# A linear attention followed by a mixture of adapters: one hand-written order of work replaced by another

## The chip, the core and the metric

The kernel runs on one core of a Trainium2 chip. A core has a matrix engine (PE, TensorE), a vector engine (DVE), an engine for functions (ACT, ScalarE), a general engine (POOL, GpSimd) and a queue engine (SP, SyncE). Each takes its own instructions strictly in order, and they meet through semaphores. Sixteen DMA engines carry data between device memory and SBUF; TensorE writes its results to PSUM, which DVE and ACT read. The metric is the device time of one execution in microseconds (us).

## What is computed

Eight batches of eight heads, 576 positions, 64 features. Queries and keys go through relu and are weighted by the cosine and the sine of their position; each head sums `kv = k_p^T v` and `z = sum k_p`, and each query row divides its numerator by its denominator. The 4608 rows of 512 then go through eight small adapters, of which the two with the highest logits count for each row.

```python
q_p, k_p = phi(q, cos_w, sin_w), phi(k, cos_w, sin_w)   # [r*c, r*s], r = max(x, 0)
kv  = einsum('bhsf,bhsd->bhfd', k_p, v)
den = einsum('bhsf,bhf->bhs', q_p, k_p.sum(2)) + 1e-6
x   = (einsum('bhsf,bhfd->bhsd', q_p, kv) / den[..., None]).transpose(0, 2, 1, 3).reshape(4608, 512)
logits = x @ w_gate                    # the top two of 8, softmax over the two: w
out = x + sum_k w[k] * (x @ A[e_k]) @ B[e_k]
```

## The kernel before

The 4608 rows are cut into 36 tiles of 128 rows, numbered n = 0 to 35; nine tiles cover two batches, and the tile in the middle of each nine (n = 4, 13, 22, 31) takes half its rows from each of the two. Batch 0 is done ahead of the order below. All else is issued one step at a time from the string `ORDER` (line 31 on): a letter names the step, numbers say which tile, batch or group, and a letter at the end (`a`, `d`, `p`) puts it on ACT, DVE or POOL. A step's instructions go to the ends of their engines' queues, so the string fixes the order on every engine at once.

For each batch b there are load steps `Dk.b`, `Dv.b`, `Dq.b` (line 131 and 140; DMAs issued by POOL, which cast f32 to bf16; a k or v comes in two parts, one of 320 KB and one of 256 KB, a q in one of 576 KB). `K b.s.i` (lines 266, 268) weights one fifth of the keys by cosine (i = 0) or sine (i = 1) on ACT or DVE. `U` (line 281) is a relu of keys on DVE for later `G b.s`, which weights on POOL with two instructions (line 271). `M b.s` (line 306) are the eight products of a fifth of a batch into `kv`, and `W b` (line 314) copies the finished `kv` out on ACT.

For each tile n: `Q` transposes the queries and weights them by cosine and sine with products against diagonal matrices (line 339, 16 products; for tiles in the list `QUAD`, line 327, 32 products of 64 by 64 that lie side by side in the quadrants of the array). `E n.gp` evacuates them with a relu on ACT (line 355) or DVE (line 357). `N` makes numerators and denominators (line 383). `R` normalises on DVE: the reciprocal (line 398) and the product (line 405). The small epsilon comes in by a product on PE, or, for tiles in `EPS_DVE`, by an addition on DVE (line 394), or, for tiles in `EPS_ACT`, by step `F` on ACT (line 366). `X` transposes the tile (line 413), `C` copies it out of PSUM on ACT or DVE (line 420), `L` multiplies it by gate and adapters (line 440). Three tiles share a gate: `A` finds the two highest logits (DVE, lines 449 to 473), `S` makes the weights (ACT), `B` applies them (DVE, line 503), `Z` transposes (line 515), and the result comes out with a `C` or with `Y` (line 520). `O` multiplies by the second adapter matrix (line 546); x itself is added by a product with the identity (line 545), or, for tiles in `ADDS`, on POOL (`P`, line 553), or, for `ADDS_DVE`, on DVE as the output is copied out. `V` copies the output out on ACT (line 564) or DVE (line 567). `T` stores it (line 577, issued by SP). `H` is a product that computes nothing used, `J` lays the adapter matrices.

Three things hold the order together across engines. The result of `N` has one PSUM place, so the next `N` waits for `R`. Buffers of keys, values and queries are used again by later batches (batch 5 takes those of batch 0 or 1, and so on), so a load waits for the last reader of the older batch. And SP, whose queue holds the stores alone, begins with one small DMA (line 625) that waits until all loads but the last `HOLD` = 2 are there; all stores stand behind it. Finished outputs wait in 24 buffers.

Of the kernel before, what the change touches and what calls it, by code (L numbers as in the profile page):

```python
# [25 lines left out]
ORDER = """
R0 H Q1.0 Q1.1 E1.0.a H X0 K1.0.1.d E1.1.a K1.1.0.d Q2.0 K1.4.0.d C0.a N1 K1.0.0.d E2.0.a
K1.2.0.d Q2.1 R1 E2.1.a H Q3.0 K1.3.0.a K1.3.1.d H N2 E3.0.d X1 K1.2.1.a Q3.1 R2 E3.1.a H H M1.3
K1.4.1.a C1.d M1.0 M1.2 K1.1.1.a N3 M1.4 R3 X2 M1.1 C2.a Q4.0 Q4.1 E4.0.a E4.1.d W1 H H H Q5.0
Q5.1 E5.0.d N4 E5.1.a X3 R4 Q6.0 Q6.1 E6.0.a C3.d H H N5 E6.1.a J Q7.0 K2.4.0.a R5 Q7.1 X4
E7.0.a L0 U2.0.2 C4.a N6 K2.3.1.d L1 G2.0 E7.1.a R6 L2 X5 K2.4.1.a Q8.0 Q8.1 A0 C5.a N7 G2.1
E8.0.a M2.4 R7 S0 M2.0 E8.1.a X6 Dq.3 K2.2.0.a M2.1 B0 N8 Dk.4 K2.3.0.a L3 R8 L4 L5 K2.2.1.a Z0
M2.3 C6.a.0 A1 Q9.0 Q9.1 M2.2 E9.0.d Dv.4 S1 E9.1.a X7 B1 Q10.0 W2 Q10.1 C7.d E10.0.a N9 X8 O0
F9 E10.1.a U3.0.2 Z1 L6 R9 O1 C8.a.1 G3.0 Q11 V0.d V1.a L7 N10 E11.0.a U3.2.3 G3.1 X9 R10 O2
E11.1.a O3 C9.a Q12.0 Q12.1 V2.d Dq.4 V3.a X10 N11 E12.0.a K3.3.1.d M3.0 G3.2 R11 K3.3.0.a M3.1  # L40
L8 E12.1.a M3.3 K3.4.0.d Dk.5 K3.4.1.a A2 M3.2 N12 M3.4 C10.d S2 F12 Q13.0 W3 B2 Q13.1 Dv.5 X11
R12 E13.0.a Z2 O4 E13.1.a O5 C11.d.2 Q14.0 V5.a N13 V4.d E14.0.a Q14.1 L9 Dq.5 K4.4.0.d F13
E14.1.a O6 R13 X12 L10 K4.4.1.a Q15 U4.0.2 C12.a N14 V6.d O7 G4.1 E15.0.a X13 R14 E15.1.a L11
Q16.0 V7.a Q16.1 G4.0 A3 C13.a N15 M4.1 E16.0.a X14 R15 E16.1.a M4.4 Dk.6 Q17.0 S3 C14.a Q17.1
B3 N16 E17.0.a X15 U4.2.3 L12 E17.1.a Dq.6 R16 O8 M4.0 C15.a G4.2 L13 K4.3.1.a V8.d Z3 L14 N17
Y3.a A4 Q18.0 K4.3.0.a Q18.1 Dv.6 M4.2 E18.0.a R17 M4.3 S4 E18.1.a X16 B4 Q19.0 W4 Q19.1
K5.4.1.d C16.a N18 U5.2.3 O9 U5.0.2 O10 E19.0.a G5.2 L15 R18 L16 E19.1.a X17 Q20.0 C17.a Q20.1
K5.4.0.d G5.1 V9.d N19 E20.0.a L17 X18 E20.1.a V10.d Z4 Q21.0 F19 G5.0 C18.a.4 Q21.1 R19 M5.4
M5.1 E21.0.a A5 N20 E21.1.a Dk.7 O11 F20 M5.2 K5.3.0.d V11.a R20 X19 O12 K5.3.1.a M5.0 V12.d S5
N21 C19.a M5.3 B5 F21 Q22 W5 R21 X20 L18 E22.0.a O13 K6.4.0.d L19 E22.1.a U6.2.4 Q23.0 U6.0.2  # L50
C20.a N22 V13.d G6.1 E23.0.a Q23.1 O14 R22 L20 E23.1.a Q24.0 Q24.1 Dv.7 A6 E24.0.a X21 Z5
E24.1.a N23 C21.d.5 Q25.0 S6 F23 Q25.1 G6.2 B6 E25.0.a O15 X22 R23 E25.1.a L21 Q26.0 C22.a Q26.1
G6.0 V14.d E26.0.a N24 X23 E26.1.a R24 Z6 O16 L22 C23.a.6 Dq.7 Q27 V16.d N25 V15.a G6.3 L23 R25
X24 K6.4.1.a M6.0 M6.1 E27.0.a P15 A7 M6.2 C24.a O17 E27.1.a N26 U7.2.4 X25 V17.a R26 M6.3 G7.3
S7 C25.a M6.4 Q28.0 W6 B7 Q28.1 T0 X26 K7.4.1.d E28.0.a N27 U7.0.2 T1 O18 E28.1.a Z7 R27 G7.0
O19 L24 V18.a T2 Q29.0 C26.a.7 Q29.1 V19.d T3 N28 G7.1 O20 E29.0.a T4 L25 R28 L26 E29.1.a O21 T5
X27 V20.a Q30.0 G7.2 C27.d Q30.1 T6 V21.a A8 N29 X28 E30.0.a T7 M7.3 C28.a R29 P17 M7.1 T8
E30.1.a M7.2 S8 T9 K7.4.0.d O22 P18 N30 B8 V22.a X29 T10 M7.0 R30 C29.a P20 M7.4 T11 Q31 W7 L27
T12 L28 E31.0.a P21 L29 T13 Z8 E31.1.a A9 Q32.0 N31 Y8.a T14 P22 E32.0.a Q32.1 R31 O23 T15 O24
E32.1.a X30 T16 S9 Q33.0 V23.a C30.d N32 B9 E33.0.a T17 P23 X31 R32 Q33.1 C31.a T18 O25 L30  # L60
E33.1.a V25.d Z9 T19 X32 V24.a N33 C32.d.9 Q34.0 T20 F33 P24 Q34.1 R33 E34.0.a L31 T21 L32 O26
E34.1.a A10 T22 X33 V26.a N34 Q35 C33.a T23 R34 P26 O27 S10 E35.0.a T24 O28 E35.1.a B10 X34 T25
N35 V27.a C34.d L33 V28.a R35 Z10 L34 T26 Y10.a O29 A11 X35 T27 V29.a O30 C35.d T28 O31 S11
V30.a B11 L35 V31.a Z11 A12 O32 T29 Y11.a V32.d S12 O33 T30 B12 O34 V33.a T31 V34.d Z12 Y12.a
T32 O35 V35.d T33 T34 T35
"""


# [1 line left out]
def kernel(ctx, tc, q, k, v, w_gate, A, Bw, out):  # L70
# [317 lines left out]
    def normalise(n):  # L388
        nd = nd_t.pop(n)[:, :, 0:4 * W].rearrange("p g (j x) -> p g j x", x=W)
        rden = p_g.tile([128, H], FP32, name="rden")  # L390
        den = nd[:, :, :, D:W]
        if n in EPS_DVE:
            den1 = p_g.tile([128, 2, 4, 1], FP32, name="den1")
            nc.vector.tensor_scalar(out=den1, in0=den, scalar1=EPS, scalar2=None, op0=ALU.add)
# [277 lines left out]
```

## Time and profile before

| what | value |
|---|---|
| three timed runs | 105.49, 110.0, 110.76 us; median 110.0 |
| the profiled execution | 105.81 us, its span 103.9 us |
| granted TensorE clock, mean over the span | 0.979 |
| busy: PE, DVE, ACT, POOL | 93.8, 85.0, 85.7, 65.8 us |
| weight loads on PE | 70.7 us |
| matmul instructions | 1764 |
| DMA: loads issued by POOL | 13.84 MB |
| DMA: SP's queue (stores and k of batch 0) | 10.62 MB |

A row of a group gives line, engine, operation, tiles, count, then busy time in us and the mean of one in ns, then the idle time of the engine just before it and what ended that. A window row gives busy time and count for PE, its weight loads (PEld), DVE, ACT and POOL, then the clock, the share of the DMA engines that was busy (over 1 where packets overlap) and what they wrote in GB/s. A timeline row gives start and length.

### The profile page before, as it was taken

What the parts mean: (1) busy time and instruction counts of PE and PEld (TensorE: products, weight loads), DVE (VectorE), ACT (ScalarE), POOL (GpSimd) and SP (SyncE); (2) the same over time, 40 slices, a digit from 0 to 9 for tenths busy, and PEclk for the clock granted to TensorE, in tenths of its full rate; (3) what the DMA queues carried; (4) which work ended last, traced back from release to release, by engine and by line L of the source; (5) the groups of instructions that cost most, each with busy time, mean ns of one, the idle gap of its engine ahead of it and who ended that gap; (6) DMA issues with size and microseconds to landing.
All of it is one profiled execution on the core that took longest, in us unless ns stands there. A gap on an engine that the chain in (4) does not pass through costs nothing.

```text
span 103.9 us, 4379 instructions
## 1 busy us (share of the span) xinstructions
PE 93.8 (90%) x1764; PEld 70.7 (68%) x1764; DVE 85.0 (82%) x302; ACT 85.7 (82%) x185; POOL 65.8 (63%) x99
## 2 busy tenths in 40 slices
PE   2999989999999999999999999899999999998600
PEld 1334866777788779768897988679878888763100
DVE  5499469558989799999989899999999989979800
ACT  4359469667999998999999999799999899997600
POOL 5996342343997599649886940999779994620000
PEclk9999999999999999999999999999999999999965
DMA  2999999999999999999999999999999999999791
GB/s 31 369 235 206 201 202 200 203 195 181 203 206 198 203 206 198 199 205 206 197 203 205 197 209 199 201 197 179 176 293 389 402 396 403 386 391 365 274 375 40
DMA packets 26997, 24.74 MB, mean 238 GB/s; under 512 B 2784, under 2 KB 21856, under 8 KB 26976
## 3 DMA queue, kind: packets, MB, share of 16 engines
q0 software_dynamic: 21248, 13.84, 90.7%
q1 hardware_dynamic: 5728, 10.62, 27.4%
q8 instruction: 14, 0.23, 0.8%
q14 instruction: 7, 0.06, 0.1%
HBM read 28.85 MB, written 9.44 MB: 368 GB/s over the span
## 4 chain that ended last, share of the span: by engine, by line
PE 41%; DMA 25%; DVE 18%; POOL 5%; issue 4%; ACT 1%; DVEq 0%; POOLq 0%
DMA v<-in_v_dram 22%; PE cd L306 9%; PE qd L339 7%; PE xz L413 6%; DVE xt L405 5%; PE nd L383 5%; PE za L440 5%; PE cd L546 4%; DMA out_dram<-osb 3%; DVE osb L567 2%; DVE xT L420 2%; DVE kp L268 2%; PE cd L545 2%; PE qd L327 1%; DVE rden L398 1%
## 5 line engine op out<-in xcount | busy, mean ns | idle before, releaser
L355 ACT ACTIVATE qpT<-qd 128x512 bf16<-128x512 f32 x67 | 38.7, 621 | 2.6 <-PE qd L339 2.2
L271 POOL TENSOR_SCALAR kp<-k,tab_kv 128x512 bf16<-128x512 bf16 x38 | 25.7, 690 | 8.3 <-PE qd L339 3.7
L405 DVE TENSOR_TENSOR xt<-nd,rden 128x512 bf16<-128x512 f32 x36 | 24.9, 691 | 2.5 <-DVE rden L398 0.5
L339 PE MATMUL qd<-diag,q 128*64 128x128 bf16 x480 | 20.6, 222 | 0.1
L306 PEld LDWEIGHTS <-kp 128*128 128x128 bf16 (+1 forms) x352 | 17.3, 96 | 2.6 <-issue 0.9
L306 PE MATMUL cd<-v,kp 128*128 128x128 bf16 (+2 forms) x312 | 17.8, 214 | 0.3
L339 PEld LDWEIGHTS <-q 128*64 128x64 bf16 x480 | 14.8, 109 | 4.4 <-issue 1.7
L420 ACT COPY xT<-xz 128x512 bf16<-128x512 bf16 (+1 forms) x25 | 16.6, 665 | 1.3 <-PE xz L413 1.1
L383 PE MATMUL nd<-kvsb,qpT 128*128 128x65 bf16 (+1 forms) x320 | 15.3, 194 | 0.7 <-DVE qpT L357 0.5
L413 PE MATMUL xz<-ident,xt 128*128 128x128 bf16 x144 | 14.2, 221 | 0.5 <-DVE xt L405 0.3
L383 PEld LDWEIGHTS <-qpT 128*128 128x128 bf16 (+1 forms) x320 | 12.0, 100 | 2.3 <-DVE xt L405 0.6
L440 PE MATMUL za<-AW,xT 128*128 128x136 bf16 x140 | 12.7, 223 | 0.0
L413 PEld LDWEIGHTS <-xt 128*128 128x128 bf16 x144 | 10.1, 115 | 3.6 <-DVE xt L405 1.9
L553 POOL TENSOR_TENSOR osb<-osb,xt 128x512 f32<-128x512 f32 x9 | 10.3, 1160 | 2.6 <-ACT osb L564 2.6
L131 POOL DMA_DIRECT2D k<-in_k_dram x14 | 9.8, 701 | 2.4 <-DMA k<-in_k_dram 2.0
L266 ACT ACTIVATE kp<-k,tab_kv 128x512 bf16<-128x512 bf16 (+1 forms) x16 | 11.2, 726 | 0.1
L131 POOL DMA_DIRECT2D v<-in_v_dram x12 | 8.4, 703 | 3.6 <-DMA v<-in_v_dram 2.6
L440 PEld LDWEIGHTS <-xT 128*128 128x128 bf16 x144 | 9.5, 98 | 1.5 <-DVE xT L420 0.3
L564 ACT COPY osb<-cd 128x512 f32<-128x512 f32 x17 | 10.0, 616 | 0.5 <-PE cd L546 0.4
L586 PE MATMUL wu<-wide,ones 128*128 128x512 bf16 x24 | 7.9, 509 | 2.1 <-DVE eps_hi L195 2.1
L140 POOL DMA_DIRECT2D q<-in_q_dram x8 | 6.3, 791 | 4.0 <-DMA q<-in_q_dram 2.2
L567 DVE TENSOR_TENSOR osb<-cd,xt 128x512 f32<-128x512 f32 x13 | 8.8, 680 | 0.0
(91 smaller groups left out, 138.7 us busy)
## 6 DMA issues: line engine op xcount, KB each, us to landing
out_dram<-osb SPq DMA_DIRECT2D x36, 256.0 KB, 4.8
q<-in_q_dram POOLq DMA_DIRECT2D x8, 576.0 KB, 11.3
k<-in_k_dram POOLq DMA_DIRECT2D x7, 320.0 KB, 10.7
v<-in_v_dram POOLq DMA_DIRECT2D x6, 320.0 KB, 11.1
k<-in_k_dram POOLq DMA_DIRECT2D x7, 256.0 KB, 10.8
v<-in_v_dram POOLq DMA_DIRECT2D x6, 256.0 KB, 11.8
k0f<-in_k_dram SPq DMA_DIRECT2D x1, 1152.0 KB, 5.5
v<-in_v_dram POOLq DMA_DIRECT2D x1, 576.0 KB, 7.7
```

The lines of the kernel that those rows point to most:

```text
L131: nc.gpsimd.dma_start(out=t[pr, :, 0:n * D], in_=x)
L266: nc.scalar.activation(dst, src, AF.Relu, bias=0.0, scale=tab)
L271: nc.gpsimd.tensor_scalar(out=dst, in0=src, scalar1=tab, scalar2=1.0, op0=ALU.mult, op1=ALU.mult)
L306: nc.tensor.matmul(out=out[:, 0:W] if b and s == NJ - 1 else out, lhsT=lhsT, rhs=rhs, start=(first and g == 0), stop=(last and g == G - 1) ...
L339: nc.tensor.matmul(out=t[cols, j, 2 * gi:2 * gi + 2, :], lhsT=q_b[b][:, 2 * gp + gi, s, :], rhs=diag[:, s, i], start=(j == 0 and gi == 0), ...
L355: nc.scalar.activation(t, src, AF.Relu)
L383: nc.tensor.matmul(out=nd[pr, gg, j * W:(j + 1) * W], lhsT=qpT[:, j, pr], rhs=kv_t[b][:, h % 2, h // 2, :], start=(eps_late(n) and j == 0) ...
L405: nc.vector.tensor_tensor(out=x, in0=nd[:, :, :, 0:D], in1=rden.rearrange("p (g j) -> p g j", g=2).to_broadcast([128, 2, 4, D]), op=ALU.mult)
L413: nc.tensor.transpose(out=xz[:, c * 128:(c + 1) * 128], in_=x[:, c], identity=ident)
L420: copy(t[:, 0:c], xz[:, 0:c * 128].rearrange("p (c s) -> p c s", c=c))
L440: nc.tensor.matmul(out=za_t[g][:, i, :], lhsT=xT[:, c, :], rhs=AW[:, c, :], start=(c == 0 and i == 0), stop=(c == DCH - 1), skip_group_che ...
L567: nc.vector.tensor_tensor(out=t, in0=src, in1=xt_t.pop(n), op=ALU.add)
```

## The change

The order is replaced, and the lists that belong to it: `EPS_DVE`, `EPS_ACT`, `QUAD`, `ADDS` and `ADDS_DVE`. No function is touched. Counted over the whole string: `QUAD` goes from six tiles to four (11, 15, 22, 27, 31, 35 become 1, 30, 31, 35), `EPS_DVE` from 22 to 27, `EPS_ACT` from 8 to 3 (and `F` steps with it), tiles whose x is added without a product from 25 to 24, of which POOL adds 10 for 9. Steps on ACT and DVE: `C` from 25 and 11 to 21 and 15, `E` from 66 and 4 to 65 and 5, `K` from 16 and 16 to 17 and 15, `V` from 20 and 16 to 22 and 14. The loads come in another order; with their places among POOL's own steps:

```
before  ... Dv.5 Dq.5 G4.1 G4.0 Dk.6 Dq.6 G4.2 Dv.6 G5.2 G5.1 G5.0 Dk.7 G6.1 Dv.7 G6.2 G6.0 Dq.7 G6.3 ...
after   ... Dv.5 G4.0 G4.1 Dk.6 G4.2 Dq.5 Dk.7 Dq.6 G5.2 G5.1 G5.0 Dv.6 G6.2 G6.1 Dq.7 Dv.7 G6.0 G7.2 G6.3 ...
```

`HOLD` stays 2, so SP's small DMA now waits for the second part of v of batch 6, where it waited for the first part of k of batch 7. The diff, cut to the lists and to the stretch around the last batch:

```diff
-EPS_DVE = [2, 3, 4, 6, 8, 10, 11, 14, 15, 16, 17, 18, 22, 24, 25, 26, 27, 28, 29, 30, 31, 34]
-EPS_ACT = [9, 12, 13, 19, 20, 21, 23, 33]
-QUAD = [11, 15, 22, 27, 31, 35]
-ADDS = [15, 17, 18, 20, 21, 22, 23, 24, 26]
+EPS_DVE = [2, 4, 5, 6, 8, 10, 11, 12, 13, 14, 15, 16, 17, 18, 19, 20, 21, 22, 24, 25, 26, 27, 28, 29, 30, 31, 34]
+EPS_ACT = [9, 23, 33]
+QUAD = [1, 30, 31, 35]
+ADDS = [15, 16, 17, 18, 19, 20, 21, 23, 25, 26]
 HOLD = 2
-ADDS_DVE = [0, 2, 4, 6, 8, 9, 10, 12, 13, 14, 16, 19, 25, 32, 34, 35]
+ADDS_DVE = [0, 3, 4, 6, 8, 10, 12, 13, 14, 22, 24, 32, 34, 35]
...
-E24.1.a N23 C21.d.5 Q25.0 S6 F23 Q25.1 G6.2 B6 E25.0.a O15 X22 R23 E25.1.a L21 Q26.0 C22.a Q26.1
-G6.0 V14.d E26.0.a N24 X23 E26.1.a R24 Z6 O16 L22 C23.a.6 Dq.7 Q27 V16.d N25 V15.a G6.3 L23 R25
...
-X27 V20.a Q30.0 G7.2 C27.d Q30.1 T6 V21.a A8 N29 X28 E30.0.a T7 M7.3 C28.a R29 P17 M7.1 T8
-E30.1.a M7.2 S8 T9 K7.4.0.d O22 P18 N30 B8 V22.a X29 T10 M7.0 R30 C29.a P20 M7.4 T11 Q31 W7 L27
...
+U6.2.4 Q22.0 Q22.1 R21 G6.2 E22.0.a X20 L18 O13 E22.1.a Q23.0 C20.a U6.0.2 N22 V13.d E23.0.a
+Q23.1 G6.1 L19 R22 E23.1.a L20 Q24.0 Q24.1 Dq.7 E24.0.a A6 Z5 X21 E24.1.a N23 Dv.7 Q25.0 C21.d.5
+S6 Q25.1 F23 E25.0.a B6 O14 X22 E25.1.a R23 O15 G6.0 L21 C22.a Q26.0 Q26.1 V14.d V15.a N24 L22
...
+K6.4.1.a R25 L23 X24 M6.0 C24.a A7 O17 P15 N26 E27.1.a M6.2 R26 M6.3 S7 T0 V17.a P16 M6.4 T1
+Q28.0 B7 W6 Q28.1 K7.4.0.d T2 X25 E28.0.a U7.0.2 N27 O18 C25.d E28.1.a O19 G7.0 T3 R27 Q29.0
...
+X27 G7.1 V21.a T7 Q30 A8 C27.a N29 T8 M7.0 E30.0.a R29 P17 M7.2 S8 T9 E30.1.a X28 O22 K7.4.1.a
+M7.3 T10 B8 P18 N30 V22.d C28.a M7.1 T11 R30 L27 P19 X29 T12 Q31 C29.a M7.4 T13 E31.1.d E31.0.a
...
```

More of the change, by code (lines that the diff above doesn't have):

```diff
@@ L31 @@
 ORDER = """
[L32 to L49, printed above, removed]
@@ L50 @@
-N21 C19.a M5.3 B5 F21 Q22 W5 R21 X20 L18 E22.0.a O13 K6.4.0.d L19 E22.1.a U6.2.4 Q23.0 U6.0.2
-C20.a N22 V13.d G6.1 E23.0.a Q23.1 O14 R22 L20 E23.1.a Q24.0 Q24.1 Dv.7 A6 E24.0.a X21 Z5
-E24.1.a N23 C21.d.5 Q25.0 S6 F23 Q25.1 G6.2 B6 E25.0.a O15 X22 R23 E25.1.a L21 Q26.0 C22.a Q26.1
-G6.0 V14.d E26.0.a N24 X23 E26.1.a R24 Z6 O16 L22 C23.a.6 Dq.7 Q27 V16.d N25 V15.a G6.3 L23 R25
-X24 K6.4.1.a M6.0 M6.1 E27.0.a P15 A7 M6.2 C24.a O17 E27.1.a N26 U7.2.4 X25 V17.a R26 M6.3 G7.3
-S7 C25.a M6.4 Q28.0 W6 B7 Q28.1 T0 X26 K7.4.1.d E28.0.a N27 U7.0.2 T1 O18 E28.1.a Z7 R27 G7.0
@@ L56 @@
-O19 L24 V18.a T2 Q29.0 C26.a.7 Q29.1 V19.d T3 N28 G7.1 O20 E29.0.a T4 L25 R28 L26 E29.1.a O21 T5
-X27 V20.a Q30.0 G7.2 C27.d Q30.1 T6 V21.a A8 N29 X28 E30.0.a T7 M7.3 C28.a R29 P17 M7.1 T8
-E30.1.a M7.2 S8 T9 K7.4.0.d O22 P18 N30 B8 V22.a X29 T10 M7.0 R30 C29.a P20 M7.4 T11 Q31 W7 L27
-T12 L28 E31.0.a P21 L29 T13 Z8 E31.1.a A9 Q32.0 N31 Y8.a T14 P22 E32.0.a Q32.1 R31 O23 T15 O24
-E32.1.a X30 T16 S9 Q33.0 V23.a C30.d N32 B9 E33.0.a T17 P23 X31 R32 Q33.1 C31.a T18 O25 L30
-E33.1.a V25.d Z9 T19 X32 V24.a N33 C32.d.9 Q34.0 T20 F33 P24 Q34.1 R33 E34.0.a L31 T21 L32 O26
@@ L62 @@
[L62 to L65, printed above, removed]
+R0 H Q1 E1.0.a E1.1.d H H X0 K1.4.1.a Q2.0 K1.1.1.d N1 K1.2.0.d E2.0.a K1.3.1.d Q2.1 R1 K1.0.1.a
+Q3.0 E2.1.a K1.0.0.d C0.d H H H N2 K1.3.0.d Q3.1 R2 E3.1.a H H M1.0 K1.2.1.a E3.0.d X1 M1.3
@@ new lines @@
+K1.1.0.a K1.4.0.d M1.2 C1.d N3 X2 R3 M1.1 Q4.0 Q4.1 E4.0.a M1.4 E4.1.d W1 H Q5.0 N4 C2.a Q5.1
+E5.0.a R4 X3 E5.1.a Q6.0 C3.a H Q6.1 K2.2.0.d E6.0.a K2.4.0.d N5 X4 E6.1.a R5 Q7.0 C4.a Q7.1
+E7.0.a J H N6 U2.0.2 E7.1.a L0 R6 L1 G2.0 K2.2.1.a L2 Q8.0 Q8.1 K2.4.1.a A0 N7 G2.1 E8.0.a X5
+M2.2 R7 K2.3.1.a M2.0 S0 C5.d E8.1.a Dq.3 M2.4 B0 X6 K2.3.0.a N8 Dk.4 L3 R8 L4 L5 Z0 Q9.0 C6.a.0
+Q9.1 A1 M2.3 E9.0.a M2.1 Dv.4 E9.1.d S1 X7 W2 B1 Q10.0 Q10.1 C7.d E10.0.a N9 L6 Z1 F9 U3.0.2
+E10.1.a X8 O0 R9 G3.0 L7 C8.a.1 O1 V0.d Q11.0 V1.a Q11.1 K3.3.1.d N10 E11.0.a U3.2.3 L8 K3.4.1.d
@@ new lines @@
+O2 E11.1.a G3.2 R10 X9 V2.a O3 Q12.0 C9.a Q12.1 V3.d G3.1 N11 K3.3.0.a X10 R11 M3.2 E12.0.a M3.3
+E12.1.a Dq.4 M3.0 A2 K3.4.0.a M3.1 Dk.5 N12 C10.d S2 M3.4 B2 Q13.0 W3 Q13.1 R12 Dv.5 X11 E13.0.a
+Z2 O4 E13.1.a O5 C11.d.2 Q14.0 V5.a V4.d Q14.1 N13 E14.0.a K4.4.0.d X12 E14.1.a U4.0.2 O6 R13
+Q15.0 G4.0 C12.a Q15.1 E15.0.a L9 L10 V6.d N14 E15.1.a L11 G4.1 R14 O7 K4.4.1.a Q16.0 V7.a Q16.1
+A3 X13 E16.0.a Dk.6 N15 E16.1.a M4.4 R15 Q17.0 C13.a M4.0 S3 E17.0.a X14 U4.2.3 O8 B3 N16 C14.a
+G4.2 Q17.1 R16 K4.3.0.a L12 L13 E17.1.a X15 L14 Dq.5 V8.d M4.1 C15.a N17 K4.3.1.a A4 Dk.7 Z3
@@ new lines @@
+Q18.0 Y3.a Q18.1 R17 E18.0.a M4.2 M4.3 E18.1.a Dq.6 X16 S4 K5.4.1.d W4 Q19.0 B4 Q19.1 C16.a N18
+K5.3.0.d L15 U5.2.3 E19.0.a O9 R18 G5.2 E19.1.a X17 L16 V9.a Q20.0 C17.d Q20.1 K5.3.1.d E20.0.a
+L17 U5.0.2 O10 N19 E20.1.a G5.1 V10.d Z4 X18 K5.4.0.a Q21.0 R19 Q21.1 C18.a.4 M5.4 G5.0 M5.2 A5
+E21.0.a N20 M5.3 E21.1.a R20 O11 Dv.6 K6.4.0.a O12 M5.1 V11.a V12.d X19 S5 M5.0 C19.a B5 N21 W5
+U6.2.4 Q22.0 Q22.1 R21 G6.2 E22.0.a X20 L18 O13 E22.1.a Q23.0 C20.a U6.0.2 N22 V13.d E23.0.a
+Q23.1 G6.1 L19 R22 E23.1.a L20 Q24.0 Q24.1 Dq.7 E24.0.a A6 Z5 X21 E24.1.a N23 Dv.7 Q25.0 C21.d.5
@@ new lines @@
+S6 Q25.1 F23 E25.0.a B6 O14 X22 E25.1.a R23 O15 G6.0 L21 C22.a Q26.0 Q26.1 V14.d V15.a N24 L22
+E26.0.a U7.2.4 X23 R24 O16 E26.1.a G7.2 Z6 Q27.0 V16.a Q27.1 C23.d.6 E27.0.a N25 M6.1 G6.3
+K6.4.1.a R25 L23 X24 M6.0 C24.a A7 O17 P15 N26 E27.1.a M6.2 R26 M6.3 S7 T0 V17.a P16 M6.4 T1
+Q28.0 B7 W6 Q28.1 K7.4.0.d T2 X25 E28.0.a U7.0.2 N27 O18 C25.d E28.1.a O19 G7.0 T3 R27 Q29.0
+V18.a Q29.1 T4 V19.a X26 Z7 L24 E29.0.a G7.3 T5 C26.d.7 N28 O20 E29.1.a L25 R28 T6 O21 V20.a L26
+X27 G7.1 V21.a T7 Q30 A8 C27.a N29 T8 M7.0 E30.0.a R29 P17 M7.2 S8 T9 E30.1.a X28 O22 K7.4.1.a
@@ new lines @@
+M7.3 T10 B8 P18 N30 V22.d C28.a M7.1 T11 R30 L27 P19 X29 T12 Q31 C29.a M7.4 T13 E31.1.d E31.0.a
+P20 L28 L29 W7 T14 Z8 A9 Q32.0 Y8.a N31 P21 T15 E32.0.a Q32.1 R31 X30 S9 T16 O23 E32.1.a Q33.0
+V23.a T17 O24 C30.d N32 E33.0.a B9 P23 T18 X31 R32 Q33.1 C31.a O25 T19 L30 E33.1.a V24.d Z9 X32
+T20 V25.a N33 C32.d.9 Q34.0 F33 P25 Q34.1 T21 R33 E34.0.a L31 L32 T22 O26 E34.1.a A10 X33 V26.a
+N34 T23 Q35 C33.a R34 P26 O27 T24 S10 E35.0.a O28 T25 E35.1.a B10 X34 N35 V27.a C34.d L33 V28.a
+R35 Z10 L34 T26 Y10.a O29 A11 X35 T27 V29.a O30 C35.d O31 T28 S11 V30.a B11 L35 V31.a Z11 A12
@@ L66 @@
+O32 T29 Y11.a V32.d S12 O33 T30 B12 O34 V33.a T31 V34.d Z12 Y12.a T32 O35 V35.d T33 T34 T35
 """
```

## The prediction

> **What bounds the kernel now.** I read the page first: span, the DMA rows of its slices, and the shares of the chain of waits.
>
> ```profile
> span 103.9 us, 4379 instructions
> ...
> DMA  2999999999999999999999999999999999999791
> GB/s 31 369 235 206 201 202 200 203 195 181 203 206 198 203 206 198 199 205 206 197 203 205 197 209 199 201 197 179 176 293 389 402 396 403 386 391 365 274 375 40
> ...
> HBM read 28.85 MB, written 9.44 MB: 368 GB/s over the span
> ...
> PE 41%; DMA 25%; DVE 18%; POOL 5%; issue 4%; ACT 1%; DVEq 0%; POOLq 0%
> ```
>
> The DMA engines never rest before the last three slices. The kernel has two DMA stages: loads move about 200 GB/s to slice 27 (twice that is read, as f32 becomes bf16), then the stores run at about 395. Only in the two slices after 70 us, and in the last three, is either rate missed. Next the windows, whose columns are PE, PEld, DVE, ACT and POOL busy, the clock, DMA share and GB/s, for the places where the rates change:
>
> ```profile
> 14.00:32.40 18.40, 18.04 (x343) 14.03 (x339) 14.70 (x46) 15.58 (x30) 10.85 (x16) 1.00 1.42 199
> ```
>
> ```profile
> 32.40:84.30 51.90, 51.13 (x1099) 42.61 (x1098) 48.29 (x163) 49.88 (x112) 41.04 (x57) 1.00 1.28 228
> ...
> 71.00:77.00 6.00, 5.85 (x117) 5.17 (x113) 5.72 (x22) 5.93 (x14) 4.88 (x7) 1.00 1.16 194
> 77.00:95.00 18.00, 17.54 (x353) 13.46 (x348) 16.27 (x59) 16.66 (x38) 12.02 (x13) 1.00 1.05 394
> 95.00:98.00 3.00, 2.49 (x15) 0.76 (x14) 2.71 (x9) 2.38 (x7) 0.00 (x0) 1.00 0.73 272
> 98.00:101.60 3.60, 0.32 (x2) 0.04 (x2) 0.42 (x1) 0.37 (x1) 0.00 (x0) 0.71 0.96 368
> ```
>
> So two limits lie close together. Between 32.4 and 84.3 PE, ACT and DVE are busy 51.1, 49.9 and 48.3 of 51.9 us. The DMA engines are full to 95 and starve a little from 95 to 98, when compute is late with outputs. Then the DMA queues: SP's timeline, and the landing times of the last loads and of some stores.
>
> ```profile
> 69.77 0.83 SPq L625 DMA_DIRECT2D first_loads<-k  x1
> 70.65 29.44 SPq L577 DMA_DIRECT2D out_dram<-osb  x36
> ```
>
> ```profile
> L131 POOL DMA_DIRECT2D v<-in_v_dram x2: 684/696/707, 66.0 to 66.8; - x2
> ...
> DMA to landing us min/median/max: 6.7/7.4/8.0
> ```
>
> ```profile
> L140 POOL DMA_DIRECT2D q<-in_q_dram x1: 807/807/807, 70.1 to 70.1; - x1
> ...
> DMA to landing us min/median/max: 9.6/9.6/9.6
> ```
>
> ```profile
> L577 SPq DMA_DIRECT2D out_dram<-osb x8: 595/686/1323, 70.7 to 76.7; - x8
> ...
> DMA to landing us min/median/max: 7.1/7.3/8.2
> ```
>
> ```profile
> L577 SPq DMA_DIRECT2D out_dram<-osb x2: 549/558/568, 98.9 to 99.5; - x2
> ...
> DMA to landing us min/median/max: 2.8/2.8/2.8
> ```
>
> SP releases the stores at 69.8, when the first part of k of batch 7 is in. Left then are k's other part, 256 KB, and v and q of 576 KB each: 1.44 MB, or 7.2 us at 200 GB/s. All 36 stores are 9.44 MB, or 24.0 us at 394. Without a hole that ends at 69.8 + 31.2 = 101.0; the last store landed at 99.5 + 2.8 = 102.3. The holes are 1.3 us: 3.0 x (1 - 272/394) = 0.9 from 95 to 98, 0.2 from 98 on, and so 0.2 from 71 to 77. For that last one bounds: 6 x 194 = 1.16 MB moved in it, 5.8 us if loads alone (0.2 lost). If two stores, 0.52 MB, were among it, 0.64/0.2 + 0.52/0.394 = 4.5 us (1.5 lost). The first stores took 7.1 to 8.2 us to land, the last ones 2.8, which speaks for at most two.
>
> **The change, part by part.** It is one new order. Of the work I need the price of each kind; these groups, by line, give busy time over count:
>
> ```profile
> L355 ACT ACTIVATE qpT<-qd 128x512 bf16<-128x512 f32 x67 | 38.7, 621 | 2.6 <-PE qd L339 2.2
> ...
> L339 PE MATMUL qd<-diag,q 128*64 128x128 bf16 x480 | 20.6, 222 | 0.1
> ...
> L420 ACT COPY xT<-xz 128x512 bf16<-128x512 bf16 (+1 forms) x25 | 16.6, 665 | 1.3 <-PE xz L413 1.1
> ...
> L266 ACT ACTIVATE kp<-k,tab_kv 128x512 bf16<-128x512 bf16 (+1 forms) x16 | 11.2, 726 | 0.1
> L553 POOL TENSOR_TENSOR osb<-osb,xt 128x512 f32<-128x512 f32 x9 | 10.3, 1160 | 2.6 <-ACT osb L564 2.6
> ...
> L564 ACT COPY osb<-cd 128x512 f32<-128x512 f32 x17 | 10.0, 616 | 0.5 <-PE cd L546 0.4
> ...
> L567 DVE TENSOR_TENSOR osb<-cd,xt 128x512 f32<-128x512 f32 x13 | 8.8, 680 | 0.0
> ...
> L268 DVE TENSOR_SCALAR kp<-k,tab_kv 128x512 bf16<-128x512 bf16 (+1 forms) x16 | 6.6, 432 | 0.3 <-DMA k<-in_k_dram 0.2
> ...
> L420 DVE COPY xT<-xz 128x512 bf16<-128x512 bf16 (+1 forms) x11 | 5.2, 471 | 0.1
> ...
> L545 PE MATMUL cd<-xt,ident 128*128 128x512 bf16 x10 | 3.8, 380 | 0.0
> ...
> L394 DVE TENSOR_SCALAR den<-nd 128x8 f32<-128x8 f32 x22 | 3.5, 157 | 1.7 <-PE nd L383 1.6
> L357 DVE TENSOR_SCALAR qpT<-qd 128x512 bf16<-128x512 f32 x5 | 3.4, 687 | 2.5 <-PE qd L339 2.5
> ...
> L327 PE MATMUL qd<-diag,q 64*64 64x64 bf16 x192 | 2.7, 195 | 0.0
> ...
> L366 ACT ACTIVATE den<-nd,eps_c 128x8 f32<-128x8 f32 x8 | 2.2, 273 | 0.1
> ```
>
> I split both orders at token Q9, which in the chain of waits stands here:
>
> ```profile
> 32.53 0.57 PE qd L339 x16
> ```
>
> Ahead of it ACT is busy 15.6 of 18.4 us (row 14 to 32.4), so relief there is worth little; I count what lies behind it, and leave out steps that only slip past the mark.
> - ACT: three copies C less, 3 x 0.66; one evacuation E, 0.58; five F (the epsilon added on ACT), 5 x 0.275. Two K more, 2 x 0.70, and two V, 2 x 0.59. Sum: -1.99 - 0.58 - 1.37 + 1.40 + 1.18 = -1.4 us.
> - DVE: three C more, 3 x 0.47; one E, 0.69; five den, 5 x 0.16; two K less, 2 x 0.41, and two V, 2 x 0.68. Sum +0.7.
> - PE: the fewer products are fewer instructions, not less time. A tile whose q goes through quadrants takes 32 x 2.7/192 = 0.45 us, one that does not 16 x 20.6/480 = 0.69. Behind Q9 three tiles lose the quadrants, +0.7. One tile more adds x by a product, +0.2 to 0.4 (0.38 by its row; overlapped with its neighbour less). Sum +1.0.
> - POOL: one add, +1.2, beside an engine busy 41.0 of 51.9 us: nothing, unless DVE meets it.
>
> That last clause has a row. Of 16 K steps on DVE one took three times the mean, beside POOL's adds:
>
> ```profile
> 81.00 1.31 DVE L268 TENSOR_SCALAR kp<-k,tab_kv 64x512 bf16<-64x512 bf16 x1
> ```
>
> ```profile
> 79.89 4.55 POOL L553 TENSOR_TENSOR osb<-osb,xt 128x512 f32<-128x512 f32 x4
> ```
>
> It began where POOL passed from one add to the next. The change puts this step (K7.4.0) ahead of POOL's long run of adds (P17 on, though just behind P16), and gives its twin K7.4.1 to ACT: DVE gets back 1.31 - 0.43 = 0.9 us, and between 0 and 0.9 of it reaches the end, as DVE has 3.6 us idle in this stretch. The Trainium skill ("SBUF — State Buffer", section "SBUF: two separate sides") has a lock on a port pair that DVE and GpSimd share, held for a whole instruction, the loser fully blocked. By that rule the one more add could cost DVE another 1.2, and its sum would be 0.7 - 0.9 + 1.2 = +1.0. The trace bears the rule out in this one row; the other 15 K steps, (16 x 0.432 - 1.31)/15 = 0.37 each, say that a meeting is rare, so I go by the row.
>
> What do these come to at 84.3? If ACT sets the pace, -1.4; if DVE, 0.7 - 0.9 = -0.2; if PE, +1.0. The chain is PE 41%, DVE 18%, ACT 1%, which is nearest to PE; but PE is called busy 51.1 of 51.9 us by modelled ends, and waits that are short do not show in it. Between the ends -1.4 and +1.0 I take 0. Behind 84.3 the two orders are nearly the same, so the shift passes on.
>
> The loads: k6 moves ahead of q5, k7 ahead of q6 and v6 (and of G5), v6 down behind G5, and q7 and v7 stand together ahead of G6.0, where the old order had q7 behind G6.0 at 70.1. On POOL an issue takes 0.7 (each part of a k or v) or 0.8 us (q), by the rows above. So G5 has the same 1.4 us ahead of it as before, k7 for v6; G6.2, now ahead of v7, comes 1.4 earlier; G6.0 waits 0.8 longer, for q7, and with it M6.0 on PE. POOL has 10.9 us idle to take that in; with no cover M6.0 would be 0.8 late. The gain of the earlier issue is the hole from 71 to 77, 0.2 to 1.5 us. But a fuller DMA there only makes the stores catch up with compute sooner, and from 95 to 98 they already wait for it. What can reach the end is the queue of the last stores:
>
> ```profile
> 98.36 0.42 DVE osb L561
> ```
>
> The last output is ready at 98.8, its store is issued at 99.5 behind others: 0 to 0.7 us, of which I take 0.3, since the stores before it still come from a late compute.
>
> SP now releases the stores on v6's last part, one load part (256 KB, 1.3 us) later in the sequence, at 71.1; all 36 stores queue behind that wait. It costs nothing as long as the loads behind it fill the DMA engines, and with holes up to 1.3 us.
>
> Sum: 0 from compute, -0.3 from the store queue. The profiled execution took 105.8 (span 103.9 and 1.9 around it); so 105.5. The three timed runs are 105.5, 110.0 and 110.8: the sum stands with the lowest, and a median of runs like the upper two would be 110 - 0.3 = 109.7.
>
> **Rivals.**
> 1. Compute moves the wrong way: PE sets the pace, +1.0, and the 0.8 us of G6.0 may come on top: 106.8 to 107.6. For it the chain's 41%; against it PE's short waits.
> 2. Both holes close and ACT set the pace: -1.3 (holes) to -2.2, the latter with loads at 209 and stores at 403 GB/s, the best slices. 103.6 to 104.5; over 2% only at the very end.
> 3. Slower by over 2%: v7 lands too late. It is now the last load, and M7.0 needs it.
>
> ```profile
> 79.63 1.53 PE L306 MATMUL cd<-v,kp 128*128 128x128 bf16 x24
> ```
>
> The old M7 products began at 79.6, with v7 there since 66.8 + 8.0 = 74.8. In the old order q7 came last and, among the stores, took from 74.8 to 79.7: 4.9 us for 576 KB that alone need 2.9. If the new last two loads share with stores from the release at 71.1 on at that pace, both are through at 71.1 + 9.8 = 80.9; in an even share, twice 2.9 us each, at 82.7. PE takes its work in order, so everything behind M7.0 waits 1.3 to 3.1 us: 107.1 to 108.9. It costs from a landing at 79.6 on, and is over 2% from 81.7. Against it: the old v7 came through at nearly full pace while stores stood issued from 70.7 on. The Trainium skill ("DMA: Bandwidth & Descriptors", section "Queues, rings and completion order") says that each DMA engine goes round its queues in turn, a packet at a time. By that rule loads and stores would share from the first store on, and the last load lands late, which is this rival; the stores' 7.1 us to the first landing speak against an even share.
> 4. Nothing comes through: 105.8.
>
> **How the numbers follow.** Forecast (104.9 to 106.2, with rival 4 in it): 0.40. Rival 1: 0.16. Rival 2: 0.20, of which 0.11 is beyond 2%. Rival 3: 0.24, of which 0.18 is beyond 2%. Two per cent, 2.1 us, is about what a measurement of this kernel can tell from no change. Faster 0.11; slower 0.18, and 0.03 for rival 1 together with a mild rival 3, 0.21; within 2% the rest, 0.68. Predicted 105.5. The low end is rival 2 in its middle, 104.0. The upper end would be rival 3's 108; but two of the three runs shown lie 4% over the profiled one for the same kernel, and a median there is 109.7, so the range goes to 110.3, rival 1 in such a run left out.
>
> **What would show it.** Right: GB/s in 71 to 77 well over 194, with q7 and v7 landed before 79; no K step on DVE over 0.6 us; N31's products within 0.5 us of 84.3; the last store issued within 0.3 us of the last output. Wrong: an idle PE in front of M7.0 with a DMA as releaser (rival 3); N31 at 85.3 with PE full (rival 1); ACT's busy share between 32 and 84 unchanged, which would deny the first sum.

## The result, and the profile after

| | median of 20 runs, us | lowest to highest, us |
|---|---|---|
| before | 106.28 | 105.42 to 112.50 |
| new order | 105.20 | 104.92 to 106.14 |

The ratio is 0.993, with a 95% interval of 0.990 to 0.995: 0.7% faster, well inside 2%. (The ratio leaves out the disturbed executions that some of the old kernel's runs are, those of 110 us and more among them, so it is not quite the ratio of the two medians.) The forecast was 105.5 within 104.0 to 110.3.

The new kernel was profiled twice. The first execution took 105.63 us, one of its slower ones, with a span of 103.9, the same as before; the second, from a later run of the same kernel, took 105.12, with a span of 103.3, and stands nearer to the median. I show the second and say where the first differs. Its page has, as for the kernel before, span, the DMA rows over 40 slices, and the chain of waits by engine:

```profile
span 103.3 us, 4301 instructions
...
DMA  2999999999999999999999999999999999998792
GB/s 30 358 242 208 200 200 200 205 197 179 203 205 198 201 208 198 199 204 207 198 198 200 207 203 201 203 184 205 198 345 402 388 397 381 391 339 341 281 383 84
...
PE 51%; DVE 21%; DMA 10%; issue 5%; ACT 4%; POOL 4%; DVEq 0%; POOLq 0%; ACTq 0%
```

The low slices after 70 us, 179 and 176 before, are 205 and 198, and the slice after them, 293 before, is 345. The windows that were shown of before (busy time and count for PE, PEld, DVE, ACT and POOL, clock, DMA share, GB/s):

```profile
32.40:84.30 51.90, 50.93 (x1045) 42.78 (x1049) 48.60 (x166) 48.74 (x105) 42.27 (x59) 1.00 1.29 233
...
71.00:77.00 6.00, 5.82 (x125) 4.94 (x121) 5.73 (x22) 5.40 (x12) 5.42 (x7) 1.00 1.27 248
77.00:95.00 18.00, 17.04 (x376) 13.71 (x374) 16.04 (x58) 16.41 (x37) 12.42 (x14) 1.00 1.00 376
95.00:98.00 3.00, 2.73 (x16) 0.83 (x14) 2.77 (x10) 2.25 (x6) 0.00 (x0) 1.00 0.79 298
```

Between 71 and 77 the DMA engines wrote 248 GB/s instead of 194. In the first execution the same window has less:

```profile
71.00:77.00 6.00, 5.86 (x115) 4.88 (x113) 5.73 (x21) 5.40 (x12) 5.09 (x7) 1.00 1.25 220
```

There a dip also stands earlier, 147 GB/s between 69 and 71 where the kernel before has 199 (184 in the second execution). Over the whole of 66 to 77 it is 196 before, 222 in the second execution and 200 in the first: there the hole has moved forward more than it has closed. From 77 to 95 it is 376 instead of 394: the best slice still has 402, so stores as such are not slower; I read it as stores that have caught up with compute and wait for it earlier. ACT fell from 49.9 to 48.7 us (48.2 in the first execution), DVE went from 48.3 to 48.6. Then the end, in two views: the last line of the chain, and the last two stores with their time to landing.

```profile
98.79 0.42 DVE osb L560
```

```profile
L576 SPq DMA_DIRECT2D out_dram<-osb x2: 539/548/556, 98.5 to 99.3; - x2
...
DMA to landing us min/median/max: 2.5/2.5/2.6
```

| us | before | new |
|---|---|---|
| last output ready | 98.78 | 99.21 |
| its store issued, after that | 0.8 | 0.1 |
| its landing, after that | 2.8 | 2.5 |
| end of span, after that | 1.6 | 1.5 |
| span | 103.9 | 103.3 |

So compute did not end sooner. What went is the queue in which the last store stood, 0.7 us, and 0.3 us of that store's own way. In the first execution both went too (issued 0.1 us after the last output, landed 2.5 later), and with a last output at 99.7 the span came out as before. The queue has one cause that can be seen, the duration of the issues on SP (shortest, middle, longest in ns). Before, then in the second new execution:

```profile
L577 SPq DMA_DIRECT2D out_dram<-osb x5: 539/556/1311, 95.5 to 98.9; - x5
...
DMA to landing us min/median/max: 2.8/2.9/3.7
```

```profile
L576 SPq DMA_DIRECT2D out_dram<-osb x5: 539/545/556, 96.0 to 98.5; - x5
...
DMA to landing us min/median/max: 2.4/2.5/2.6
```

One issue, begun at 96.2, took 1.31 us instead of 0.55, and the four behind it never caught up: that is the whole 0.8. Issues of 1.0 us and more stand in every trace, one to six of the 36; in the two new executions the last one began at 90.5 and 90.7, early enough to be made up for. Stores that land sooner here fit DMA engines that are less behind, but what makes an issue long, and whether the new order keeps it away from the end, no run shows.

Why is the last output 0.4 us later? In the chains of waits of before and of the first new execution, in this order, the rest hangs on one load, the second part of v of batch 2:

```profile
18.91 10.32 DMA v<-in_v_dram
```

```profile
19.06 10.98 DMA v<-in_v_dram
30.18 1.40 PE cd L305 x24
```

It landed at 29.2 before and at 30.0 in the first new execution; in the second it was issued at 18.9 and took 10.7, so 29.5. From that landing to the last output it is 69.6, 69.7 and 69.7 us: 98.78 - 29.23, 99.70 - 30.04 and 99.21 - 29.55. By these sums the new order computes at the same pace as the old one, to 0.1 us, and what differs between executions is when that load came in. The chain of the second execution does not name the load, because it goes by the modelled end of the product before; but in all fourteen traces of this case the products that need it begin 0.04 to 0.22 us after its landing. That it sets the end is still argued: no run moved it alone. Nor is it shown that the order has no part in it: it landed at 29.1 to 29.2 in the three traces of the old order, at 29.1 to 30.2 in the eleven of the new one and its variants.

### The profile page after: what moved, and what is told of

It is laid out like the page before. It is cut to its first block, busy times and chain, and to the rows that moved or that the text cites. A ratio compares the mean times of both kernels' runs of the same rounds, so it can differ in the third digit from the quotient of the medians.

```text
span 103.9 us, 4315 instructions
## 1 busy us (share of the span) xinstructions
PE 94.3 (91%) x1733; PEld 70.5 (68%) x1733; DVE 86.2 (83%) x309; ACT 83.3 (80%) x178; POOL 67.0 (64%) x100
## 4 chain that ended last, share of the span: by engine, by line
PE 46%; DMA 22%; DVE 15%; POOL 5%; issue 4%; ACT 3%; POOLq 0%; DVEq 0%; ACTq 0%
DMA v<-in_v_dram 22%; PE cd L305 11%; PE qd L338 9%; PE xz L412 6%; PE za L439 6%; PE nd L382 5%; DVE xt L404 4%; PE cd L545 4%; DVE osb L566 2%; DVE xT L419 2%; PE cd L544 2%; DVE k L280 1%; POOL k L130 1%; PE xz L514 1%; DVE rden L397 1%
## 5 line engine op out<-in xcount | busy, mean ns | idle before, releaser
L354 ACT ACTIVATE qpT<-qd 128x512 bf16<-128x512 f32 x66 | 37.9, 623 | 5.2 <-PE qd L338 3.9
L270 POOL TENSOR_SCALAR kp<-k,tab_kv 128x512 bf16<-128x512 bf16 x38 | 25.7, 689 | 10.2 <-DVE den L393 3.7
L338 PE MATMUL qd<-diag,q 128*64 128x128 bf16 x512 | 22.4, 223 | 0.3 <-DMA q<-in_q_dram 0.2
L338 PEld LDWEIGHTS <-q 128*64 128x64 bf16 x512 | 15.9, 109 | 5.9 <-issue 3.2
L419 ACT COPY xT<-xz 128x512 bf16<-128x512 bf16 (+1 forms) x21 | 13.7, 653 | 2.3 <-PE xz L514 1.2
L552 POOL TENSOR_TENSOR osb<-osb,xt 128x512 f32<-128x512 f32 x10 | 11.4, 1154 | 2.6 <-ACT osb L563 2.6
L265 ACT ACTIVATE kp<-k,tab_kv 128x512 bf16<-128x512 bf16 (+1 forms) x17 | 12.3, 728 | 0.1
L563 ACT COPY osb<-cd 128x512 f32<-128x512 f32 x20 | 11.7, 614 | 0.6 <-PE cd L545 0.5
L419 DVE COPY xT<-xz 128x512 bf16<-128x512 bf16 (+1 forms) x15 | 7.3, 484 | 0.6 <-PE xz L412 0.4
## 6 DMA issues: line engine op xcount, KB each, us to landing
v<-in_v_dram POOLq DMA_DIRECT2D x6, 320.0 KB, 10.7
```

The costliest lines, as they stand in the source:

```text
L265: nc.scalar.activation(dst, src, AF.Relu, bias=0.0, scale=tab)
L270: nc.gpsimd.tensor_scalar(out=dst, in0=src, scalar1=tab, scalar2=1.0, op0=ALU.mult, op1=ALU.mult)
L338: nc.tensor.matmul(out=t[cols, j, 2 * gi:2 * gi + 2, :], lhsT=q_b[b][:, 2 * gp + gi, s, :], rhs=diag[:, s, i], start=(j == 0 and gi == 0), ...
L354: nc.scalar.activation(t, src, AF.Relu)
L419: copy(t[:, 0:c], xz[:, 0:c * 128].rearrange("p (c s) -> p c s", c=c))
L563: nc.scalar.copy(t, src)
```

## The experiments

Eleven variants ran. Ratios are to the kernel before, run beside them on the same chip. The new kernel was run once more beside three of them, `HOLD` = 1 and the two that take work off ACT:

> The new kernel unchanged, beside the three others of this call on the same chip: 0.990 to 0.996 of before.

Measured 0.991 (0.987 to 0.994), median 105.15 us: the result stands.

**The places of the loads.** First alone, in the old order:

```diff
-  ... Dq.5 G4.1 G4.0 Dk.6 ... Dq.6 ... G4.2 ... Dv.6 ... G5.0 Dk.7 ... G6.1 Dv.7 G6.2 G6.0 ... Dq.7
+  ... G4.1 G4.0 Dk.6 ... G4.2 ... Dq.5 Dk.7 Dq.6 ... G5.0 Dv.6 ... G6.1 Dq.7 Dv.7 G6.2 G6.0
```

> The old order with the new places of the loads alone (k6, k7, q5, q6, v6, q7, v7). My theory: the hole from 71 to 77 us closes (GB/s there 210 to 225 instead of 194), q7 and v7 are in by 79, and the end moves with the queue of the last stores only, ratio to before 0.993 to 0.998. Rival, the loads are the whole gain: 0.993 or less. Rival, v7 is now too late for M7: over 1.01, with PE idle in front of M7.3. If the even spread of the new kernel's times comes from the loads, no run here lies over 107.

Measured 0.997 (0.993 to 1.001), 105.40 to 106.59 us in 12 runs. The windows from 71 and from 95 us:

```profile
71.00:77.00 6.00, 5.95 (x113) 5.20 (x116) 5.69 (x21) 5.93 (x14) 4.89 (x8) 1.00 1.27 251
95.00:98.00 3.00, 2.64 (x15) 0.75 (x13) 2.80 (x9) 2.48 (x7) 0.00 (x0) 1.00 0.79 296
```

The hole closes with the loads alone, 251 GB/s (225 over 66 to 77), and M7 is not held up: v7 is in at 78.0, and the products begin at 79.9. The last output is ready at 99.0, its store is issued 0.3 us later, behind an issue of 0.8 us, and lands after 2.8. So in this execution half a microsecond of the queue is gone with the loads alone, where my theory had it, though an interval that reaches 1.001 does not show the whole to be a gain. Then the reverse, the new order with the old places of the loads:

```diff
-  ... G4.0 G4.1 Dk.6 G4.2 Dq.5 Dk.7 Dq.6 G5.2 G5.1 G5.0 Dv.6 G6.2 G6.1 Dq.7 Dv.7 G6.0 ...
+  ... Dq.5 G4.0 G4.1 Dk.6 Dq.6 G4.2 Dv.6 G5.2 G5.1 G5.0 Dk.7 G6.2 Dv.7 G6.1 G6.0 Dq.7 ...
```

> The new order with the loads in the old places. My theory: the hole from 71 to 77 is back (GB/s under 200) and the gain shrinks to between 0.995 and 1.000 of before. Rival, the gain is from compute: still 0.993. If the loads make the even spread, runs over 107 come back here.

Measured 1.005 (1.002 to 1.008): slower than before, and 0.012 above the new kernel, more than any theory had. The chain of waits tells why, and the window beside it:

```profile
61.49 9.94 DMA k<-in_k_dram
...
71.56 0.43 DVE k L280
```

```profile
71.00:77.00 6.00, 5.11 (x106) 4.44 (x103) 5.17 (x20) 4.64 (x11) 4.66 (x6) 1.00 1.19 230
```

The new order has the relu U7.2.4 on DVE much earlier, before R24; there it now waits for k of batch 7, which comes in at 71.4, and everything behind it on DVE waits too. PE, DVE and ACT are all idle 0.8 to 1.4 of 6 us here, and the last output is ready at 100.7 instead of 99.2. The hole came back in part only, 230 GB/s where I had expected under 200, so I put the loss down to the late k7 more than to the hole. The earlier loads are two things: they fill the hole, and they carry the rest of the new order, which is laid out on k7 being there by 65 us. No time lies over 107 us in either kernel (105.40 to 106.59 and 106.40 to 106.97 us), so the places of the loads alone do not decide the spread.

**When the stores are released.** `HOLD` decides it; the new order has 2, and one of my rivals was that loads and stores would share the DMA engines evenly and v7 come too late.

```diff
-HOLD = 2
+HOLD = 4
```

> The new order with the stores released with four loads left (q6, v6, q7 and v7, once k7 is in, at about 64.5 us) instead of two (71.4). My third rival, loads and stores in an even share: the four loads of 2.36 MB take twice 11.8 us, v7 lands at 85 to 88 instead of 78 to 79, M7.0 waits on PE until then, and the ratio to before is 1.03 to 1.06. If loads go ahead of stores as they seemed to in the old trace, v7 lands at 79 to 81 and the ratio is 0.993 to 1.005.

Measured 1.081 (1.075 to 1.087): the rival's mechanism, beyond its own price. The two parts of v7 as issued by POOL with their time to landing, the windows while both kinds move and the one in which PE is busy for a third of the time, and the chain:

```profile
L130 POOL DMA_DIRECT2D v<-in_v_dram x2: 709/710/712, 67.2 to 67.9; - x2
...
DMA to landing us min/median/max: 16.7/18.4/20.0
```

```profile
72.00:78.00 6.00, 4.01 (x44) 3.77 (x45) 2.31 (x13) 2.43 (x5) 3.63 (x5) 0.72 1.15 286
78.00:84.00 6.00, 5.78 (x135) 4.58 (x133) 5.39 (x20) 5.17 (x12) 4.24 (x7) 1.00 1.17 299
84.00:90.00 6.00, 1.91 (x19) 1.94 (x20) 1.49 (x5) 1.49 (x4) 5.34 (x5) 0.82 1.03 347
```

```profile
67.93 20.02 DMA v<-in_v_dram
88.09 1.87 PE cd L305 x16
```

v7 is through at 87.9, at the upper end of the 85 to 88 that I had put on an even share. Half of the 200 GB/s of loads and half of the 395 of stores would be 298 together, by an estimate from the rates above; measured are 286 and 299. PE waits for v twice, 2.1 us for v6 and 4.3 us for v7; it takes its work in order, and behind it the outputs stop too, so that the DMA engines then starve at 125 GB/s from 90 to 96. That last part was in no expectation. Now the other way:

```diff
-HOLD = 2
+HOLD = 1
```

> The new order with the stores released with one load left (v7, once q7 is in, at about 74.3 us instead of 71.4). The DMA engines have loads to fill them meanwhile, so v7 lands at 77 instead of 78 to 79 and nothing waits for it either way. If only the sum of bytes counts: 0.991 to 0.997, as the new kernel. If the first stores need some 6 us from issue to landing whatever else goes on, a hole comes between loads and stores and the ratio rises to 0.998 to 1.015.

Measured 1.011 (1.005 to 1.017). The stores' first issue is at 74.7, and the windows around it:

```profile
74.00:75.00 1.00, 1.00 (x26) 0.84 (x25) 0.96 (x3) 0.70 (x3) 1.00 (x2) 1.00 1.43 205
75.00:76.00 1.00, 0.95 (x27) 0.79 (x22) 1.00 (x4) 1.00 (x4) 0.49 (x1) 1.00 0.53 68
76.00:77.00 1.00, 1.00 (x19) 0.61 (x19) 0.93 (x4) 1.00 (x3) 0.92 (x2) 1.00 0.85 284
```

Its first stores, as issued and with their time to landing:

```profile
L576 SPq DMA_DIRECT2D out_dram<-osb x4: 601/631/883, 74.7 to 77.0; - x4
...
DMA to landing us min/median/max: 2.8/3.1/3.1
```

There is a hole here, 68 GB/s between 75 and 76. Until 75 the one load left, v7, keeps up the 200 GB/s of loads by itself (q7 landed at 73.8); but at 74.7 it is mostly through, and the stores are not there yet. My reason had the wrong size: I had put it on some 6 us that the first stores need in any case. They land 3 us after their issue here, against 7.1 to 8.2 us in the kernel before: most of that time comes from the loads still queued. In this run compute ends at 98.9; the stores are what ends late, the last one issued 1.7 us after its output.

**The engines' sums.** Does PE set the pace, so that fewer or more tiles through quadrants matter? The new order with four more of them:

```diff
-QUAD = [1, 30, 31, 35]
+QUAD = [1, 11, 15, 22, 27, 30, 31, 35]
-  ... Q11.0 ... Q11.1 ... Q15.0 ... Q15.1 ... Q22.0 Q22.1 ... Q27.0 ... Q27.1 ...
+  ... Q11 ... Q15 ... Q22 ... Q27 ...
```

> The new order with tiles 11, 15, 22 and 27 through quadrants again beside 1, 30, 31 and 35: PE saves 4 x 0.24 = 0.96 us behind Q9. If PE sets the pace, compute ends 0.7 to 1.0 us earlier and the ratio to before is 0.985 or so, 0.007 under that of the new kernel. If quadrants only save time that PE then waits, it is 0.993, as the new kernel. Slower than the new kernel, 0.997 or more, if a tile in quadrants makes its evacuations wait for one another, since both its halves are done only at its end.

Measured 0.994 (0.989 to 0.998), as the new kernel: 0.96 us of PE saved for nothing. From the landing of v2 to the last output its trace has 69.8 us, no less than the new kernel's 69.7. Then about as much work added to one engine at a time, each step doubled in its place so that the result is the same:

```diff
-  ... X14 ... X16 ... X18 ... X20 ... X22 ...
+  ... X14 X14 ... X16 X16 ... X18 X18 ... X20 X20 ... X22 X22 ...
```

> The new order with five transposes of x done twice (X14, X16, X18, X20, X22; same result): 5 x 0.22 = 1.1 us more on PE between 47 and 66 us. If PE sets the pace, compute ends 0.9 to 1.1 us later and the ratio to before rises from the new kernel's 0.993 to 1.002. If PE has short waits to take it in, 0.993 to 0.997. I expect the latter, since eight quadrant tiles instead of four gave nothing.

```diff
-  ... K4.4.0.d ... K5.4.1.d ... K5.3.0.d ... K5.3.1.d ...
+  ... K4.4.0.d K4.4.0.d ... K5.4.1.d K5.4.1.d ... K5.3.0.d K5.3.0.d ... K5.3.1.d K5.3.1.d ...
```

> The new order with four key steps of DVE done twice (K4.4.0, K5.4.1, K5.3.0, K5.3.1; same result): 4 x 0.37 = 1.5 us more on DVE between 45 and 62 us. If DVE sets the pace, 1.002 to 1.007 of before; if its 3.3 us of idle time take it in, 0.993 to 0.997.

```diff
-  ... K4.4.1.a ... K4.3.1.a ...
+  ... K4.4.1.a K4.4.1.a ... K4.3.1.a K4.3.1.a ...
```

> The new order with two key steps of ACT done twice (K4.4.1, K4.3.1; same result): 2 x 0.72 = 1.4 us more on ACT between 47 and 54 us. If ACT sets the pace, 1.002 to 1.006 of before; if its idle time (3.7 us of 51.9) takes it in, 0.993 to 0.997, which I expect.

| added | ratio to before (95%) | over the new kernel's 0.993, us | landing of v2 to last output, us (new kernel: 69.7) |
|---|---|---|---|
| PE, 1.1 us | 0.995 (0.991 to 0.999) | 0.3 | 70.1 |
| DVE, 1.5 us | 0.996 (0.992 to 1.000) | 0.4 | 70.3 |
| ACT, 1.4 us | 1.003 (0.999 to 1.008) | 1.1 | 71.1 |

The third column is the difference of the ratios by 106 us; the last comes from one execution each. The intervals of PE and DVE overlap the new kernel's; ACT's does not. The new kernel's ratio is from another chip; among themselves the three stood on one, with medians of 105.9, 106.2 and 106.6 us. ACT's work comes through for three quarters, and I had expected ACT to take it in. So here the engine that the chain of waits hardly names (4%) is the one whose delay reaches the end. One rival is not tested: ACT's two steps lie between 47 and 54 us, DVE's and PE's are spread over 45 to 66, so it may be the place that is sensitive and not the engine. (In the trace with more work on PE an issue of 1.54 us on SP begins at 97.7, and the last store stands 1.0 us in the queue again.) Would taking work off ACT help, then?

```diff
-  ... K4.4.1.a ... K4.3.1.a ...
+  ... K4.4.1.d ... K4.3.1.d ...
```

> The new order with K4.4.1 and K4.3.1 on DVE instead of ACT: ACT has 1.4 us less, DVE 0.7 us more. Twice these two steps on ACT cost 0.010. If ACT sets the pace in this stretch, the ratio is 0.983 to 0.989. If the engines are so balanced that what ACT gives up is lost to DVE or PE, it is that of the new kernel, 0.991 to 0.995, or worse.

Measured 0.995 (0.992 to 0.999), not faster than the new kernel's 0.991 beside it. Further in the same direction:

```diff
-  ... K4.4.1.a ... K4.3.0.a ... K4.3.1.a ... K5.4.0.a ... K6.4.0.a ...
+  ... K4.4.1.d ... K4.3.0.d ... K4.3.1.d ... K5.4.0.d ... K6.4.0.d ...
```

> The new order with K4.3.0, K5.4.0 and K6.4.0 on DVE too: ACT has 3.6 us less, DVE 1.8 us more. If ACT sets the pace throughout, 0.970 to 0.985, but no further than where the stores stand without a hole, some 0.98. If DVE becomes the pace, 0.993 or worse.

Measured 1.002 (0.999 to 1.005). Its chain of waits by engine:

```profile
PE 37%; DVE 36%; DMA 10%; issue 7%; POOL 3%; ACT 2%; DVEq 0%; POOLq 0%; ACTq 0%
```

DVE went from 21% of the chain to 36%. That alone says little, for the shares move between executions of one kernel (the new one's two have 15% and 21% for DVE). From the landing of v2 to the last output the two runs have 70.2 and 71.2 us instead of 69.7: what ACT gave up, and more, was lost elsewhere. That it was lost on DVE is argued. No version here beats the new kernel.

**The step that POOL's adds blocked.** In the old order:

```diff
-  ... K7.4.1.d E28.0.a ... T9 K7.4.0.d O22 ...
+  ... K7.4.1.d K7.4.0.d E28.0.a ... T9 O22 ...
```

> The old order with one step moved: K7.4.0 on DVE right behind K7.4.1, ahead of POOL's adds, where it took 1.31 us. It should take 0.35 to 0.45 us there. If the 0.9 us reaches the end, the ratio is 0.992; if DVE's idle time swallows it, 0.998 to 1.000, which is what I expect.

Measured 1.002 (0.997 to 1.006): nothing, as expected. In the trace the two K steps together took 0.60 us at 75.1, and the DVE work that stood behind the step at 82 came about 1 us earlier (R30 began at 81.7 instead of 82.7); the last output was ready at 98.65 instead of 98.78. DVE's idle time between 82 and the end swallowed the rest. In the new kernel the step is this one, which took no more than 0.45 us although an add of POOL's (P16) ran until about 75.75:

```profile
75.45 0.45 DVE L267 TENSOR_SCALAR kp<-k,tab_kv 64x512 bf16<-64x512 bf16 x1
```

## Why the prediction was right, point by point

The forecast was 0.3 us less, from the store queue alone; measured is 0.7 less.

- **Compute, 0 between -1.4 and +1.0.** Within the bounds: the last output came 0.4 us later in the second execution and 0.9 in the first, 0.1 in both once the landing of v2 is taken out. That load was in no term of the sum. The reason for the 0 was poor, and that it came out so near is in part luck. I put PE nearest to the pace by its 41% of the chain; added work, at its places, shows PE and DVE to be the more forgiving engines and ACT the one that passes a delay on. And the 1.4 us taken off ACT (measured 49.9 to 48.7, so 1.1) did not come back as time; f1, with two more steps off ACT, gained nothing either. Sums per engine gave the right bounds and no more.
- **PE's +1.0.** It did not reach the end: eight tiles through quadrants or four, the time is the same.
- **K7.4.0.** 0.9 us back on DVE (measured 0.9, from 1.31 to 0.45), none of it at the end.
- **The hole from 71 to 77.** It closed, by 248 GB/s against 194, and in e1 with the loads alone; in the first execution it closed by half, 220, with a new dip ahead of it.
- **The store queue, -0.3 of at most -0.7.** The place was right and the size too small: the queue before the last store went from 0.8 to 0.1 us, all of it, and the landing of that store, which I had not counted, from 2.8 to 2.5. I had taken it for stores that stand one behind another, and less than the whole because the stores before it come from a late compute; the trace shows one long issue on SP behind it, 1.31 us, and that none came so late in the two new executions is not shown to be the order's doing. These two are 1.0 us; the later last output took 0.4 of it in this execution, which leaves the 0.6 between the two spans.
- **The later release, at no cost if the engines stay full.** Right for `HOLD` = 2 (q7 and v7 fill them, see the rows below), wrong one step further, where the last load is mostly through when the first store is issued.
- **Rival 3, v7 too late.** The share is real once stores move (v7 took 20.0 us with `HOLD` = 4, 10.2 with 2 and 9.4 with 1). The Trainium skill's rule ("DMA: Bandwidth & Descriptors", section "Queues, rings and completion order"), that each DMA engine goes round its queues in turn, agrees with the 20.0. But it does not bite here. The issue of v7 and its time to landing, M7.0 on PE, and the windows behind the first store's issue, in the second new execution:

```profile
L130 POOL DMA_DIRECT2D v<-in_v_dram x2: 709/710/712, 67.4 to 68.1; - x2
...
DMA to landing us min/median/max: 8.8/9.5/10.2
```

```profile
79.91 1.06 PE L305 MATMUL cd<-v,kp 128*128 128x128 bf16 x16
```

```profile
72.00:75.00 3.00, 3.00 (x60) 2.75 (x56) 2.79 (x15) 2.49 (x5) 3.00 (x5) 1.00 1.35 198
75.00:76.00 1.00, 1.00 (x29) 0.91 (x28) 1.00 (x4) 0.93 (x3) 0.76 (x1) 1.00 1.28 310
76.00:78.00 2.00, 1.95 (x43) 1.48 (x41) 1.77 (x6) 2.00 (x5) 1.66 (x3) 1.00 1.07 383
```

v7 is in at 68.1 + 10.2 = 78.3, and M7.0 begins at 79.9: 1.6 us in hand. The first store is issued at 72.1, but until 75 the rate is that of loads alone; only then do store bytes move, and the first store lands at 78.4. So the loads had the engines to themselves for 3 us after the release, and that is what the price of this rival left out.
- **Signs named beforehand.** All held in the second execution: N31's products began at 84.66, 0.3 us after the old ones. In the first they began at 85.16, 0.8 after, with v2 0.8 us late and PE busy 51.7 of 51.9 us. That is outside the sign that I had named and close to the one for rival 1 (85.3 with PE full); its time of 106.8 did not come, as the store's part gave back what compute lost.

## What to carry to other kernels

When two resources, here DMA and compute, end close to one another, look at what stands between the last output and its store, issue by issue: here one long issue held all of that time. Of the three moments tried for letting the stores in, two loads from the end was the best: one load later left a hole and cost 1.8%, two loads earlier made the matrix engine wait and cost 8.8%; three loads were not tried. And an engine's share of the chain of waits did not tell which engine passes a delay on: doubling a harmless step on each engine in turn tells more, best at the same places in the order.
